# Two blocks of a retention layer loaded as 32x32 blocks and transposed on VectorE instead of TensorE

## The chip, the cores and the metric

The kernel runs on one core of a Trainium2 chip. A core has a matrix engine (TensorE, PE in the profile, with PEld for its weight loads), a vector engine (VectorE, DVE), a scalar engine (ScalarE, ACT), GpSimd (POOL) and a queue engine (SyncE, SP) that issues the transfers between HBM and the on-chip memory. Each engine runs its own instructions in the order of the program, and they wait for each other through semaphores. The metric is the device time of the launch in microseconds.

## The reference

q, k and v are float32 arrays of 8 batches x 8 heads x 576 positions x 64. For every batch and head

    ret = (q @ k.T / sqrt(64)) * D        D[i, j] = gamma_h ** (i - j) where i >= j, else 0
    attn = ret @ v

The heads are then laid side by side, which gives x with 4608 tokens of 512 numbers, and a feed-forward block follows:

    h = max(x @ w1, x @ w2, x @ w3)       512 -> 768
    out = h @ w_out                       768 -> 512

The four weights come as float64; they are made float32 on the chip.

## The kernel before

The 4608 tokens are cut into 36 blocks of 128 tokens (g = 0 to 35, C = 128) and 9 tiles of four blocks. The loop at the end of the kernel calls ffn(t), the feed-forward of tile t, and between its parts it puts the steps that steps(t + 1) lists for the blocks of the next tile. So while tile 0 goes through its feed-forward, blocks 4 to 7 go through the retention; the code calls these four a, b, c, d. That stretch is the one that the change touches. No scheduler moves anything: the order of the calls is the order on each engine.

**Tile 0's feed-forward.** The weights are loaded in 256 KB transfers as 64-bit words (`load_weights`, L610, tile name bits; the output weights L605 in transfers of 512 KB), two row groups to a buffer, with four buffers. `convert_all` turns each into float32: four ScalarE operations (L778, L779, L785, L788) and four VectorE operations (L786 frac, L791 mant, L795 expo, L803 w). The products come in nine units of two row groups (fp, i), called unit 0 to 8 here: each is 2 x 4 matmuls of 128x512 (`up_plain`, L934), followed by a maximum on VectorE (L939) or a copy on ScalarE (L941). Then come the products with w_out (L921). A float32 matmul shows as two instructions in the trace. When a buffer of words has been converted, it can be loaded again: the words of unit n + 4 wait for the conversion of unit n. Units 9 to 11 of this order are the output weights, called out0 to out2 here.

**Blocks 4 and 5 (a and b).** Their q, k and v are each loaded in 256 KB, or in two halves where a block lies across two batches, as block 4 does (L259). q and k are transposed on TensorE, 4 + 4 instructions a block (L295), and copied from PSUM by ScalarE (L296). `parity_scores` makes the scores of each half of 64 tokens on its own (L322) and the products of keys and values that carry the state from one half to the next (L327); VectorE masks the scores (L338) and sums the states (L346 to L350). `parity_values` takes the outputs from them (L506, L497); in the middle of it, two one-column copies on ScalarE (L510) stand between its first and its second group of products with the old states.

**Blocks 6 and later (c, d and on).** k is loaded twice: plainly (kraw), and with q in blocks of 32x32 (`load_blocks`, L241, tiles kxraw and qraw; 16 transfers of 32 KB a block, with runs of 128 bytes). VectorE transposes the 32x32 blocks, one instruction for k and one for q (L221, STREAM_TRANSPOSE). `chunk_scores` (L377, L380), a mask (L384), state sums on VectorE (L392) and GpSimd (L394) and `chunk_values` (L528, L535) do what the parity functions do for a and b, on other layouts of the same sizes. `carry` (L408) puts the state that the earlier form left into the layout of the later one.

**The queue.** Every load is issued by SP, in the order of the calls. The transfers of SP use eight semaphores in turn. The next transfer on a semaphore waits until the last one on it has landed, so a transfer cannot be issued before the one eight places ahead of it in the order has landed. An instruction that reads a tile waits for the semaphores of all the transfers that fill it; the transposes of a block's k and q wait for all 16.

Of the kernel before, what the change touches and what calls it, by code (L numbers as in the profile page):

```python
# [40 lines left out]
FP32 = mybir.dt.float32  # L41
# [10 lines left out]
NH = NT // 2  # L52
BY_PE = 6
BY_CHUNKS = 6
AHEAD = 3
# [44 lines left out]
def kernel(  # L100
# [23 lines left out]
    CPT = NT // C  # L124
    assert B * S % C == 0 and S % D == 0 and BY_CHUNKS % 2 == 0 and S >= C and N % NT == 0 and NT % P == 0 and 2 * D == P and NP == NDC

# [56 lines left out]
    assert all(start_of(g) in (0, None) for g in range(CPT))  # L183
    low = raw0.tile([P, D], FP32, name="low")
    for c in range(2):
        nc.gpsimd.tensor_copy(low[half(c)], causal[half(c), half(c)])


    raws, vds, qks, sts, states, mids, kvs, stacks = {}, {}, {}, {}, {}, {}, {}, {}

# [32 lines left out]
    def load_blocks(g, *blocks):  # L223
        for n, src in (("q", q), ("kx", k)):

            if 0 in blocks:
                shape = [P, NP, C // 32, 32] if g < BY_CHUNKS else [P, H, D // 32, 32]
                raws[n, g] = raw.tile(shape, FP32, tag=n, name=n + "raw", bufs=2)
            t = raws[n, g]
            for blk in blocks:  # L230
                b, pos = divmod(g * C + 32 * blk, S)
                if g < BY_CHUNKS:
                    for a in range(4):
                        nc.sync.dma_start(
                            t[32 * a:32 * a + 32, :, blk, :],
                            src[b, a // 2::2, pos:pos + 32, 32 * (a % 2):32 * (a % 2) + 32].rearrange("p j i -> j p i"))
                    continue
                c, e = divmod(blk, 2)
                for a in range(2):
                    r = D * c + 32 * a  # L240
                    nc.sync.dma_start(  # L241
                        t[r:r + 32, :, e, :],
                        src[b, :, pos:pos + 32, 32 * a:32 * a + 32].rearrange("h p i -> p h i"))
# [17 lines left out]
    def decay(g):  # L261
        factor = gk[:].unsqueeze(2).to_broadcast([C, H, D])
        t = raws.pop(("v", g))
        if spread or g >= CPT + 2:
            vds[g] = t
            scaling.extend(partial(nc.scalar.mul, t[:, h, :], t[:, h, :], gk[:, h:h + 1]) for h in range(H))
            return
        vds[g] = vpool.tile([C, H, D], FP32, tag="s", name="vd")
        engine = nc.gpsimd if g < CPT - 1 else nc.vector
        engine.tensor_tensor(vds[g][:], t[:], factor, op=ALU.mult)  # L270
# [4 lines left out]
    def transposes(g, names="kq"):  # L275
        both = qks.setdefault(g, {})
        if both:
            pass
        elif g >= BY_CHUNKS:
            for n, tag in (("k", "kT"), ("q", "m1")):  # L280
# [9 lines left out]
        for n in names:  # L290
            src = raws["k", g] if n == "k" else raws.pop(("q", g))
            pool, tag = (ps_r, "r") if g >= CPT else (ps_x, "x")
            pt = pool.tile([P, NP, C], FP32, tag=tag, name=n + "t")
            for p in range(NP):
                nc.tensor.transpose(pt[:, p, :], pair(src, p), ident[:C, :C])  # L295
            nc.scalar.copy(both[n][:], pt[:])  # L296

    def scores(g):
        chore(len(urgent))
        scale(len(scaling))  # L300
        if g >= CPT:
            (chunk_scores if g >= BY_CHUNKS else parity_scores)(g)
            return
# [6 lines left out]
        for j in range(2):  # L310
            st = sts[g, j] = att.tile([C, NP, C], FP32, tag=f"m{j}", name="st", bufs=2 + j)
            soon(partial(nc.vector.tensor_tensor, st[:], s[j][:],
                         causal[:].unsqueeze(1).to_broadcast([C, NP, C]), op=ALU.mult))

    def parity_scores(g):

        qT, kT, kr, vd = qks[g]["q"], qks[g]["k"], raws.pop(("k", g)), vds[g]
        rows = [ps_r.tile([P, 2, NP, D], FP32, tag="r", name=f"s{j}") for j in range(2)]
        kept = [c for c in range(2) if place(g, c) < S // D - 1]

        def score(p, j, c):
            nc.tensor.matmul(rows[j][half(c), 0, p, :], lhsT=kT[half(j), p, half(c)], rhs=qT[half(j), p, half(c)],  # L322
                             start=True, stop=True)

        def key_value(p, j, c):
            if c in kept:
                nc.tensor.matmul(rows[c][half(j), 1, p, :], lhsT=kr[half(c), 2 * p + j, :],  # L327
                                 rhs=vd[half(c), 2 * p + j, :], start=True, stop=True)

        for p in range(NP):  # L330
            for n in range(2):
                score(p, 0, n)
                score(p, 1, 1 - n)
                key_value(p, 1 - n, 0)
                key_value(p, n, 1)

        def mask(j):
            nc.vector.tensor_tensor(st[:, j::2, :], rows[j][:, 0], low[:].unsqueeze(1).to_broadcast([P, NP, D]),  # L338
                                    op=ALU.mult)

        def keep_parity(c):

            kv, factor = rows[c][:, 1], gs[:].unsqueeze(2).to_broadcast([P, NP, D])
            new = mids[g] if c == 0 else states[g + 1]
            if place(g, c) > 0:
                nc.vector.tensor_tensor(new[:], kv, (mids if c else states)[g][:], op=ALU.add)  # L346
                if c:
                    nc.vector.tensor_tensor(new[:], new[:], factor, op=ALU.mult)
            elif c:
                nc.vector.tensor_tensor(new[:], kv, factor, op=ALU.mult)  # L350
            else:
                nc.vector.tensor_copy(new[:], kv)

        st = sts[g] = att.tile([P, H, D], FP32, tag="m0", name="m", bufs=2)
        for j in range(2):
            soon(partial(mask, j))
        for c in kept:
            (states if c else mids)[g + c] = ppool.tile([P, NP, D], FP32, tag="part", name="state")
            soon(partial(keep_parity, c))

# [85 lines left out]
    def values(chunks, new_states=(), later=False, middle=()):  # L446
# [8 lines left out]
        if chunks[0] >= CPT:  # L455
            (chunk_values if chunks[0] >= BY_CHUNKS else parity_values)(chunks, t, i)
            return
# [27 lines left out]
        finish()  # L485

    def parity_values(chunks, t, i):
        o = [ps_r.tile([P, len(chunks), NP, D], FP32, tag="r", name="o") for _ in range(2)]
        cross = ((0, 0), (1, 1), (0, 1), (1, 0))

        def old(n):
            for b, g in enumerate(chunks):
                for u in range(0, NP, 2):
                    for j, c in cross:
                        m = j ^ n
                        if place(g, m) > 0:
                            nc.tensor.matmul(o[m][half(c), b, u + j, :],  # L497
                                             lhsT=(mids if m else states)[g][half(j), head(c, u) // 2, :],
                                             rhs=qks[g]["q"][half(j), head(c, u) // 2, half(m)],
                                             start=False, stop=True, skip_group_check=True)  # L500

        for b, g in enumerate(chunks):
            for u in range(NP):
                for m, c in cross:
                    h = head(c, u)
                    nc.tensor.matmul(o[m][half(c), b, u, :], lhsT=vds[g][half(m), h, :], rhs=sts[g][half(m), h, :],  # L506
                                     start=b == 0 and u == 0, stop=place(g, m) == 0, skip_group_check=True)
        old(0)
        for m in range(2):
            nc.scalar.copy(first[:], o[m][:, 0, 0, 0:1])  # L510

        def rest():
            old(1)
            between.append(partial(chunk_output, o, chunks, t, i))

        between.append(rest)

    def finish_values(_):
        between.pop()()

# [443 lines left out]
    def ffn(t):  # L964

        h = hpool.tile([P, NF, NT], FP32, tag="h", name="h")
        if t == 0:
            a, b, c, d = range(CPT, 2 * CPT)
            middles = {units[2]: [(transposes, a)], units[3]: [(scores, a)], units[5]: [(scores, b), (chunk_constants,)],
                       units[8]: [(transposes, d)]}  # L970
# [138 lines left out]
    def steps(t):  # L1109
# [12 lines left out]
        if t == 1:  # L1122
            a, b, c, d = range(CPT, 2 * CPT)
            at(0, (load, a, "kq"))
            at(1, (load, a, "v"))
            at(2, (load_weights, 2), (load, b, "kq"))
            at(3, (decay, a), (load, b, "v"), (load, c, "k"))
            at(4, (transposes, b), (load, c, "v"))
            at(5, (decay, b), (load, d, "kv"))
            at(6, (decay, c), (load_blocks, c, 0, 1, 2, 3))  # L1130
            at(7, (values, [a, b]), (finish_values, b), (decay, d), (convert, 2), (load_blocks, d, 0, 1, 2, 3))
            at(8, (transposes, c), (carry, c))
            at(9, (load, d + 1))
# [73 lines left out]
```

## Time and profile before

| | |
|---|---|
| median of 3 runs | 739.23 us (738.79 to 740.75) |
| the profiled execution | 738.46 us, with a span of 736.7 us |
| TensorE busy | 731.4 us, 99% of the span |
| VectorE busy | 572.3 us, 78% |
| ScalarE busy | 354.6 us, 48% |
| bytes moved | 59.38 MB, mean 81 GB/s |
| granted TensorE clock | 1.00 |

The page divides the span into 40 slices of 18.4 us and gives for each the busy share of each engine in tenths. The chain that ended last is followed back from the last instruction. A timeline lists instructions in the order of time: the start in us from the start of the span, how long they took, the engine, the line, what is written and read, and how many were merged into the row; in brackets stands the idle time of the engine before the row and what ended it. A row of SP tells how long the issue took, not the transfer. A table of windows gives for each stretch the busy time of each engine with the instructions begun in it, the granted clock, the busy share of the 16 DMA engines (over 1 where packets of one engine overlap) and the bytes per second.

### The profile page before, as it was taken

The numbers are of one execution on the slowest core, as the hardware profiler recorded it, in microseconds if no ns is written. First come the engines' busy times: TensorE is split into PE (matmuls) and PEld (weight loads), VectorE is DVE, ScalarE is ACT, GpSimd is POOL, SyncE is SP. The second block draws the span as 40 slices with busy tenths as digits, with TensorE's granted clock in tenths as the row PEclk, the third lists the DMA queues.
The fourth block names the chain that finished last, engine by engine and source line by source line (L and its number), as shares of the span: only waits on it lengthen the run. The fifth ranks groups of instructions, "written<-read, shape, count | busy, mean of one in ns | idle before, by whom it ended". The sixth has DMA issues, their size and how long they took to land.

```text
span 736.7 us, 17316 instructions
## 1 busy us (share of the span) xinstructions
PE 731.4 (99%) x6932; PEld 604.1 (82%) x6932; DVE 572.3 (78%) x1051; ACT 354.6 (48%) x740; POOL 39.1 (5%) x44
## 2 busy tenths in 40 slices
PE   9999999999999999999999999999999999999998
PEld 7654457888888888888888888888888888888887
DVE  5998799999886995689668866887768866893676
ACT  4886915444345525543364425543555245424441
POOL 2000010132000100010000000000100010000000
PEclk9999999999999999999999999999999999999999
DMA  9999554314251415151424243322514150000001
GB/s 222 264 233 247 107 98 115 67 27 91 73 100 27 91 42 105 37 97 32 103 52 79 45 109 60 64 53 64 109 29 88 46 125 6 1 31 28 1 1 57
DMA packets 233264, 59.38 MB, mean 81 GB/s; under 512 B 214496, under 2 KB 231904, under 8 KB 233184
## 3 DMA queue, kind: packets, MB, share of 16 engines
q1 hardware_dynamic: 232208, 58.24, 36.5%
q8 instruction: 54, 0.88, 0.5%
q14 instruction: 26, 0.21, 0.1%
q10 hardware_dynamic: 976, 0.04, 0.1%
HBM read 48.80 MB, written 9.44 MB: 79 GB/s over the span
## 4 chain that ended last, share of the span: by engine, by line
PE 97%; SPq 1%; DMA 1%; issue 0%; ACT 0%; DVE 0%
PE a L909 20%; PE b L909 17%; PE c L909 9%; PE up L934 9%; PE di L755 7%; PE d L909 6%; PE e L909 6%; PE dhc L755 5%; PE deg L755 3%; PE sk L377 3%; PE down L921 3%; PE o L528 2%; PE o L535 2%; PE dfd L755 2%; PE dx L662 1%; SPq L259 1%
## 5 line engine op out<-in xcount | busy, mean ns | idle before, releaser
L897 DVE TENSOR_TENSOR part<-part 128x512 f32<-128x512 f32 x168 | 117.9, 702 | 86.5 <-ACT part L894 83.9
L894 ACT COPY part<-b 128x512 f32<-128x512 f32 x120 | 70.3, 586 | 163.3 <-PE b L909 161.6
L897 DVE TENSOR_TENSOR h<-h,part 128x512 f32<-128x512 f32 x120 | 83.3, 694 | 24.0 <-ACT h L894 20.0
L894 ACT COPY part<-a 128x512 f32<-128x512 f32 x96 | 56.3, 586 | 51.6 <-PE a L909 51.1
L209 ACT ACTIVATE vraw<-vraw,gk 128x64 f32<-128x64 f32 x240 | 76.9, 347 | 6.6 <-DMA vraw<-in_v_dram 6.6
L909 PE MATMUL b<-s,n 128*128 128x256 f32 x288 | 73.9, 379 | 0.0
L934 PE MATMUL up<-xT,w 128*128 128x512 f32 (+2 forms) x160 | 63.5, 553 | 0.0
L909 PEld LDWEIGHTS b<-s,n 128*128 128x128 f32 x288 | 54.7, 190 | 7.4
L394 POOL TENSOR_TENSOR s<-s,gs_of 64x512 f32<-64x512 f32 x23 | 25.0, 1089 | 553.6 <-DVE s L392 476.5
L934 PEld LDWEIGHTS up<-xT,w 128*128 128x128 f32 x160 | 28.6, 190 | 30.1 <-issue 27.0
L909 PE MATMUL c<-xT,w 128*128 128x256 f32 x192 | 51.3, 389 | 0.0
L744 ACT COPY k<-di 128x256 f32<-128x256 f32 x49 | 18.3, 373 | 68.5 <-PE di L755 43.4
L909 PE MATMUL d<-s,w 128*128 128x256 f32 x192 | 49.8, 380 | 0.0
L909 PE MATMUL b<-xT,n 128*128 128x256 f32 x192 | 49.3, 379 | 0.0
L909 PE MATMUL a<-s,w 128*128 128x256 f32 x192 | 49.3, 379 | 0.0
L909 PE MATMUL a<-xT,w 128*128 128x256 f32 x192 | 49.3, 379 | 0.0
L909 PE MATMUL e<-xT,w 128*128 128x256 f32 x192 | 45.4, 379 | 0.0
L909 PE MATMUL a<-xT,n 128*128 128x256 f32 x192 | 45.4, 379 | 0.0
L909 PEld LDWEIGHTS e<-xT,w 128*128 128x128 f32 x192 | 36.5, 190 | 5.4 <-issue 0.5
L909 PEld LDWEIGHTS b<-xT,n 128*128 128x128 f32 x192 | 36.5, 190 | 5.0
L909 PEld LDWEIGHTS a<-s,w 128*128 128x128 f32 x192 | 36.5, 190 | 5.0
L909 PEld LDWEIGHTS a<-xT,w 128*128 128x128 f32 x192 | 36.5, 190 | 5.0
(196 smaller groups left out, 1382.1 us busy)
## 6 DMA issues: line engine op xcount, KB each, us to landing
bits<-in_moe_w_dram SPq DMA_DIRECT2D x36, 256.0 KB, 6.2
kraw<-in_k_dram SPq DMA_DIRECT2D x32, 256.0 KB, 3.1
vraw<-in_v_dram SPq DMA_DIRECT2D x32, 256.0 KB, 3.6
qraw<-in_q_dram SPq DMA_DIRECT2D x240, 32.0 KB, 2.1
kxraw<-in_k_dram SPq DMA_DIRECT2D x240, 32.0 KB, 2.1
out_dram<-osb SPq DMA_DIRECT2D x56, 128.0 KB, 1.7
bits<-in_moe_w_out_dram SPq DMA_DIRECT2D x6, 512.0 KB, 5.7
out_dram<-osb SPq DMA_DIRECT2D x7, 256.0 KB, 2.0
```

What stands on the lines that cost most here:

```text
L209: scaling.popleft()()
L377: nc.tensor.matmul(s[half(c), h, :], lhsT=kT[half(c), h, :], rhs=qT[half(c), h, :], start=True, stop=True)
L394: nc.gpsimd.tensor_tensor(new, new, factor, op=ALU.mult)
L528: nc.tensor.matmul(o[m][half(c), n, u, :], lhsT=vds[g][half(m), h, :], rhs=sts[g][half(m), h, :], start=n == 0 and u == 0, stop=place(g, m ...
L535: nc.tensor.matmul(o[m][half(c), n, u, :], lhsT=stacks[g][half(m), h, :], rhs=qks[g]["q"][half(m), h, :], start=False, stop=True, skip_gro ...
L744: nc.scalar.copy(place, a)
L755: nc.tensor.matmul(banks[chain], lhsT=hidden(h, order, b, late_ones)[:, e], rhs=late["V"][v][:, e], start=begins and e == 0, stop=chain no ...
L894: nc.scalar.copy(of[step], ps[step[0]][:])
L897: nc.vector.tensor_tensor(of[dst], a, b, op=op)
L909: nc.tensor.matmul(ps[chain][:, e, :], lhsT=factor(w, 2 * fp + e), rhs=xS[t][x], start=n == 1 and e == 0, stop=ends, skip_group_check=True)
L921: nc.tensor.matmul(b[:], lhsT=h[:, fb, m * P:(m + 1) * P], rhs=w_sb["out", fb], start=fb == blocks[0], stop=fb == blocks[-1])
L934: nc.tensor.matmul(ps[:, a:b], lhsT=w_sb[i, fb][:, dc * P:(dc + 1) * P], rhs=xT[t][:, dc, a:b], start=dc == 0 and a == 0, stop=dc == NDC - ...
```

## The change

Blocks 4 and 5 take the form of the later blocks. BY_PE goes from 6 to 4 and BY_CHUNKS goes away, and with it `parity_scores`, `parity_values` and what served them alone (the mask low, the dictionary mids, finish_values, one of the two load shapes). No new function is written: `load_blocks`, the VectorE transposes, `chunk_scores` and `chunk_values` now serve blocks 4 to 7 too. `carry`, from the state that block 3 leaves, is called for block 4 in place of block 6. The keys' decay of a and b is multiplied into the loaded tile itself; it stays one VectorE operation. In tile 0's feed-forward the scores of a move from unit 3 to unit 5, where those of b already stood, and now both stand between the two row groups of that unit; the small constants move from unit 5 to unit 2.

On the queue the order of the weights' loads among themselves is the same. What stands between them is moved: before, q, k and v of a and b were spread over four places; after, all of a's loads that are not k and v stand in one place, 16 transfers between the words of unit 4 and those of unit 5, and all of b's loads, k, v and 16 transfers, stand between the words of unit 7 and those of unit 8. The queue has 702 transfers in place of 673.

```diff
-BY_PE = 6
-BY_CHUNKS = 6
+BY_PE = 4
...
     def decay(g):
...
-        if spread or g >= CPT + 2:
+        if CPT <= g < CPT + 2:
+            vds[g] = t
+            nc.vector.tensor_tensor(t[:], t[:], factor, op=ALU.mult)
+            return
+        if g >= CPT:
...
     def scores(g):
...
-            (chunk_scores if g >= BY_CHUNKS else parity_scores)(g)
+            chunk_scores(g)
...
-            (chunk_values if chunks[0] >= BY_CHUNKS else parity_values)(chunks, t, i)
+            chunk_values(chunks, t, i)
...
-            middles = {units[2]: [(transposes, a)], units[3]: [(scores, a)], units[5]: [(scores, b), (chunk_constants,)],
+            middles = {units[2]: [(chunk_constants,)], units[3]: [(carry, a)], units[5]: [(scores, a, b)],
                        units[8]: [(transposes, d)]}
...
-            at(0, (load, a, "kq"))
-            at(1, (load, a, "v"))
-            at(2, (load_weights, 2), (load, b, "kq"))
-            at(3, (decay, a), (load, b, "v"), (load, c, "k"))
-            at(4, (transposes, b), (load, c, "v"))
-            at(5, (decay, b), (load, d, "kv"))
-            at(6, (decay, c), (load_blocks, c, 0, 1, 2, 3))
-            at(7, (values, [a, b]), (finish_values, b), (decay, d), (convert, 2), (load_blocks, d, 0, 1, 2, 3))
-            at(8, (transposes, c), (carry, c))
+            at(0, (load, a, "kv"))
+            at(1, (load_blocks, a, 0, 1, 2, 3))
+            at(2, (load_weights, 2))
+            at(3, (load, b, "kv"), (load_blocks, b, 0, 1, 2, 3), (decay, a))
+            at(4, (transposes, a))
+            at(5, (load, c, "kv"), (decay, b), (transposes, b))
+            at(6, (load, d, "kv"), (decay, c), (load_blocks, c, 0, 1, 2, 3))
+            at(7, (values, [a, b]), (decay, d), (convert, 2), (load_blocks, d, 0, 1, 2, 3))
+            at(8, (transposes, c))
```

More of the change, by code (lines that the diff above doesn't have):

```diff
@@ L124 @@
     CPT = NT // C
-    assert B * S % C == 0 and S % D == 0 and BY_CHUNKS % 2 == 0 and S >= C and N % NT == 0 and NT % P == 0 and 2 * D == P and NP == NDC
+    assert B * S % C == 0 and S % D == 0 and BY_PE == NT // C and S >= C and N % NT == 0 and NT % P == 0 and 2 * D == P and NP == NDC
     const = ctx.enter_context(tc.tile_pool(name="const", bufs=1))
@@ L183 @@
     assert all(start_of(g) in (0, None) for g in range(CPT))
[L184 to L189, printed above, removed]
+    raws, vds, qks, sts, states, kvs, stacks = {}, {}, {}, {}, {}, {}, {}
     def spans(g):
@@ L226, in load_blocks @@
             if 0 in blocks:
-                shape = [P, NP, C // 32, 32] if g < BY_CHUNKS else [P, H, D // 32, 32]
-                raws[n, g] = raw.tile(shape, FP32, tag=n, name=n + "raw", bufs=2)
+                raws[n, g] = raw.tile([P, H, D // 32, 32], FP32, tag=n, name=n + "raw", bufs=2)
             t = raws[n, g]
@@ L231, in load_blocks @@
                 b, pos = divmod(g * C + 32 * blk, S)
[L232 to L237, printed above, removed]
                 c, e = divmod(blk, 2)
@@ L278, in transposes @@
             pass
-        elif g >= BY_CHUNKS:
+        elif g >= BY_PE:
             for n, tag in (("k", "kT"), ("q", "m1")):
@@ L291, in transposes @@
             src = raws["k", g] if n == "k" else raws.pop(("q", g))
-            pool, tag = (ps_r, "r") if g >= CPT else (ps_x, "x")
-            pt = pool.tile([P, NP, C], FP32, tag=tag, name=n + "t")
+            pt = ps_x.tile([P, NP, C], FP32, tag="x", name=n + "t")
             for p in range(NP):
@@ L313, in scores @@
                          causal[:].unsqueeze(1).to_broadcast([C, NP, C]), op=ALU.mult))
[L315 to L359, printed above, removed]
     def begins(g):
@@ L485, in values @@
         finish()
[L487 to L519, printed above, removed]
     def chunk_values(chunks, t, i):
```

## The prediction

> **What bounds the kernel now.** First the page's chain that ended last: it is TensorE almost throughout.
>
> ```profile
> PE 97%; SPq 1%; DMA 1%; issue 0%; ACT 0%; DVE 0%
> ```
>
> Second the page's slices: TensorE is full from the second slice on, and the DMA engines are full through the first four (to 74 us), which is where blocks 4 and 5 are loaded.
>
> ```profile
> PE   9999999999999999999999999999999999999998
> DMA  9999554314251415151424243322514150000001
> ```
>
> Third TensorE's timeline of that stretch. Rows follow each other without idle time, so an instruction less is time won, and a wait is time lost.
>
> ```profile
> 40.32 0.60 PE L295 MATMUL kt<-ident,kraw 128*128 128x128 f32 x4
> 40.76 0.60 PE L295 MATMUL qt<-ident,qraw 128*128 128x128 f32 x4
> 41.20 7.03 PE L934 MATMUL up<-xT,w 128*128 128x512 f32 x16
> ...
> 64.05 0.27 PE L322 MATMUL s<-qT,kT 64*64 64x64 f32 x2
> ...
> 76.62 0.64 PE L497 MATMUL o<-qT,state 64*64 64x64 f32 x24
> 77.53 0.68 PE L497 MATMUL o<-qT,state 64*64 64x64 f32 x24 [0.27 <-ACT first L510]
> ```
>
> The 0.27 is the only wait there. Fourth the queue and its transfers. Eight loads of q blocks take 5.58 us to issue when they stand behind large loads, because each waits for the transfer eight places ahead; the eight of kx behind them take 3.90, 0.49 each, and land 2.1 us after their issue (second fence, asked for 71 to 75 us). A 256 KB load on an emptied queue takes about 3 us (third, 96.5 to 97.9 us). The last line is the windows' row for 36 to 48 us: a full DMA moves 252 GB/s.
>
> ```profile
> 35.93 6.81 SPq L610 DMA_DIRECT2D bits<-in_moe_w_dram  x8
> ...
> 65.47 5.58 SPq L241 DMA_DIRECT2D qraw<-in_q_dram  x8
> 71.09 3.90 SPq L241 DMA_DIRECT2D kxraw<-in_k_dram  x8
> ```
>
> ```profile
> kxraw<-in_k_dram SPq DMA_DIRECT2D x8, 32.0 KB, 2.1
> ```
>
> ```profile
> kraw<-in_k_dram SPq DMA_DIRECT2D x1, 256.0 KB, 2.9
> ```
>
> ```profile
> 36.00:48.00 12.00, 12.00 (x35) 5.58 (x33) 11.19 (x15) 11.94 (x13) 0.00 (x0) 1.00 1.14 252
> ```
>
> Last VectorE: two idle times where it waits for TensorE, and what a transpose pair costs (0.63 + 0.67, from start to start).
>
> ```profile
> 57.29 0.69 DVE L939 TENSOR_TENSOR h<-h,up 128x512 f32<-128x512 f32 x1 [2.62 <-PE up L934]
> ...
> 60.72 0.69 DVE L939 TENSOR_TENSOR h<-h,up 128x512 f32<-128x512 f32 x1 [0.81 <-PE up L934]
> ...
> 86.67 0.70 DVE L221 STREAM_TRANSPOSE kT<-kxraw 128x512 f32<-128x512 f32 x1
> 87.30 0.67 DVE L221 STREAM_TRANSPOSE qT<-qraw 128x512 f32<-128x512 f32 x1
> ```
>
> **The change part by part.** *TensorE, won.* The transposes of a and b go: 40.32 to 41.20 and 52.78 to 53.65, 1.76 us. Scores: parity took 48.16 to 49.24 and 64.05 to 65.14, 2.17; two chunk scores, c and d, took 92.07 to 94.11, 2.04; 0.13 won. Outputs: parity_values took 75.64 to 78.14, 2.50 with its wait; chunk_values took 101.18 to 103.20, 2.02; 0.48 won. Together 2.37 us.
>
> *ScalarE* loses four copies of 0.59 and the two of 0.16; carry (0.80) moves. *VectorE* gains two pairs of transposes, 2.6 us; masks and states of a and b cost 3.23 before (0.76 + 0.41 + 0.76 + 0.88 + 0.42) and about 3.48 after (0.69 + 0.69, 0.69 + 1.41). These 2.9 us fit into the 3.4 us of idle time above; without that cover they would cost at most as much. *GpSimd* gains one product of about 1 us (L394), with 75 us idle before its first. The decay is the same 0.68 us. All these I take as nothing.
>
> *The queue: when do b's blocks land?* A 256 KB load takes 262,144 B / 252 GB/s = 1.04 us. The weight load issued at 23.18 landed 7.1 later, at 30.3. After the change: k and v of a, 512 KB, to 32.4; six weight loads to 38.6; now a's eighth q block waits for the last of these, and eight kx at 0.49 follow it, to 42.5. In that time the queue of bytes runs empty. The next weight load is issued at 43.0 and lands 3.0 later, 46.0; eleven more to 57.4; k and v of b to 59.5; its eighth q block waits for that, eight kx to 63.4, landing at 65.5. The same reckoning of the order before gives 60.5 for the last weight load of units 0 to 8; issued at 56.48, it landed 5.3 later, at 61.8. So I add the 1.3 that it falls short: 66.8. VectorE's transposes of b: 68.1.
>
> *The first wait.* TensorE comes to the scores of b at 64.05 - 1.76 - 1.08 (a's scores, no longer at unit 3) + 1.02 (now just ahead) = 62.2. It waits 68.1 - 62.2 = 5.9 us. Behind the waiting transpose on VectorE stand the last steps of unit 6's weights (1.22 + 1.23, ready at 70.6); TensorE wants them after b's scores and half a unit (1.0 + 3.5), at 72.6: covered. Before this, unit 5's weights land at about 50.4 and are ready about when TensorE comes for them (60.52 - 2.84 = 57.7); a wait there would come off the 5.9, not on top.
>
> *The second wait.* Behind b's blocks stand unit 8's weights, out0, k and v of c, out1, k and v of d, c's blocks, out2, d's blocks. With kx of b issued at 64.7: a weight load at 65.2 lands at 68.2, three more at 71.3. Then 3.15 MB at 315 GB/s (the windows' 60 to 70 us, with such loads): 81.3. c's eight kx: 85.2. out2's second load, issued at 86.1, lands 4.9 later as before (75.53 to 80.46): 91.0. d's eight kx 94.9, landed 97.0, transposed 98.3. TensorE comes to the scores of d at 92.07 - 2.37 + 5.9 + 1.0 = 96.6, and waits 1.7. Before, d was transposed at 91.7 for 93.05.
>
> Later, VectorE is full from 95 to 134 us. The product at 117.90 reads a sum that ended at 115.69, 2.2 us of room; VectorE comes out of d's transposes 6.6 late and TensorE 5.2, so 0.8 is left. Nothing is added.
>
> Sum: -2.37 + 5.9 + 1.7 = +5.2. The profiled execution took 738.46 (736.7 and 1.8 around it): 743.7. It stands 0.8 below the median, against which I predict 744.4.
>
> *Ends.* First wait: at 276 GB/s (20 to 30 us), 0.09 less for each of 22 loads, and without the 1.3: 2.6; at 234 (30 to 35 us): 7.7. I take 252, the stretch of the same loads. Second: zero, if out2 and d come in time; at 252 GB/s for the 3.15 MB, 4.2. Sum from +0.2 to +9.5.
>
> *A rule against it.* The granted clock is 1.00 in every slice, and after 16 us no wait of TensorE is over 0.3 us; so no row shows what a long one does. The Trainium skill, TensorE: Matmul & The Clock Gate, section "What's actually happening", says that an idle window of about 3.4 us halves the clock until a busy window of that length. By that, an estimate from this page, the first wait could cost up to 1.7 us more; no run here shows it yet, and the sum leaves it out.
>
> **Rivals.** *Hidden: faster.* If b's last block landed by 60.9 (62.2 less 1.3) and d's in time, only the 2.37 would show: 736.1 against the profile, 736.9 against the median. The price turns at that landing, 5.9 us sooner. For it: small loads could overtake large ones. Against it: c's first seven q blocks, issued behind out1, took 3.7 us to land at the median in place of 2.1; and the twelve weight loads would have to come at 0.6 us each, 430 GB/s, where the best five microseconds of the trace (60 to 65) show 335.
>
> *One wait alone: about even.* With the low end of the first wait and none at d: 739.4. For it: 276 GB/s was seen with weights alone. Against it: at 36 to 48, weights nearly alone, it was 252.
>
> *More waits: over +8.* A DMA at 234 GB/s lengthens both waits: about 748.7. For it: a gap like that at 30 to 35 us may come again; the 128-byte runs may slow the weights. Against it: the queue holds only eight transfers, so the small ones pass between.
>
> **How the numbers follow.** Both waits 0.60; one wait or small ones 0.18; more 0.13; hidden 0.09. A measurement tells 0.3%, 2.2 us, from no change. Hidden is faster: 0.09. Of "one wait", 0.10 lies within 0.3%, and 0.01 of the likeliest: same 0.11. Slower 0.80. The likeliest's own range is 741.5 to 747. The range takes the ends, +0.2 to +9.5: 739.4 to 748.7; it leaves out the hidden case and what is beyond, under 2 in 10.
>
> **What would show it.** Right: L295 gone after 20 us; SP's timeline with 16 block loads between the weights and a DMA share well under 1 in their second half, at about 40 to 45 and 60 to 64 us; VectorE idle some 5 us before a transpose of kx, released by a DMA; TensorE idle 3 to 7 us before L322 of the new file at 62 us, and up to 4 at about 96. Wrong: TensorE without a gap there, or the DMA full through 40 to 65 us, which would put b's blocks earlier; a granted clock under 1 would add what the sum leaves out.

## The result and the profile after

The changed kernel takes 750.98 us at the median of six runs (750.34 to 754.35) against 739.24 us for the kernel before (738.71 to 740.75): a ratio of 1.0171, with a 95% interval from 1.0157 to 1.0186. It is 11.7 us slower; the prediction was +5.2, and its range ended at 748.7.

The profiled execution took 754.35 us with a span of 752.3 us, 15.6 more than the span before. It is one of the two longest of the six; the other four spans lie between 748.3 and 749.2 us. First the page's slices and its chain that ended last.

```profile
PE   8996979999999999999999999999999999999998
...
PEclk9998989999999999999999999999999999999999
DMA  9987753513242424332342325141515151001001
...
PE 91%; SPq 3%; DVE 3%; DMA 2%; issue 1%; ACT 0%; DVEq 0%
```

A slice is 18.8 us. TensorE is no longer full in the fourth and the sixth (56 to 75 and 94 to 113 us), the granted clock falls in the same two, and the chain now passes through SP's queue and VectorE. From the first product of tile 1 to the last matmul both kernels take 616.5 us. Of the 15.6 us, 15.0 lie in tile 0: from its first product of the feed-forward to the first of tile 1 it is 96.35 us before and 111.36 after. Most of the rest is that the stretch begins 0.3 us later (21.02 in place of 20.68).

Next TensorE's waits (us in total, times, longest) and, from its timeline, the three rows that waited over 0.5 us in that stretch.

```profile
PE sk L322 <- DVE qT L216: 8.1, 2, 5.3
PE up L845 <- ACT mant L690: 2.9, 1, 2.9
```

```profile
60.86 6.73 PE L845 MATMUL up<-xT,w 128*128 128x512 f32 x8 [2.86 <-ACT mant L690]
...
71.48 0.27 PE L322 MATMUL sk<-qT,kT 64*64 64x64 f32 x2 [2.81 <-DVE qT L216]
...
105.46 0.48 PE L322 MATMUL sk<-qT,kT 64*64 64x64 f32 x4 [5.29 <-DVE qT L216]
```

It waits for the weights of unit 5, for b and for d. VectorE's timeline tells what these were waiting for: the words of unit 5, which it could begin at 52.38 and had made into weights at 60.7, and the block loads of b and of d.

```profile
52.38 0.69 DVE L697 TENSOR_SCALAR frac<-bits 128x1024 int32<-128x1024 int32 x1 [2.91 <-DMA bits<-in_moe_w_dram]
...
59.48 1.23 DVE L714 TENSOR_TENSOR w<-mant,expo 128x1024 f32<-128x1024 f32 x1
...
70.12 0.71 DVE L216 STREAM_TRANSPOSE kT<-kxraw 128x512 f32<-128x512 f32 x1 [5.68 <-DMA kxraw<-in_k_dram]
...
104.01 0.71 DVE L216 STREAM_TRANSPOSE kT<-kxraw 128x512 f32<-128x512 f32 x1 [5.93 <-DMA qraw<-in_q_dram]
```

So all three are late loads. SP's timeline shows the queue, and the windows what the DMA engines did meanwhile (the last two numbers of a row are their busy share and GB/s, the one before is the granted clock). In both fences the first row is of the kernel before, the others are of the changed one.

```profile
81.89 3.77 SPq L241 DMA_DIRECT2D kxraw<-in_k_dram  x8
...
35.30 5.33 SPq L229 DMA_DIRECT2D qraw<-in_q_dram  x8
40.68 4.41 SPq L229 DMA_DIRECT2D kxraw<-in_k_dram  x8
45.20 7.92 SPq L521 DMA_DIRECT2D bits<-in_moe_w_dram  x12
...
57.57 6.48 SPq L229 DMA_DIRECT2D qraw<-in_q_dram  x8
64.09 3.90 SPq L229 DMA_DIRECT2D kxraw<-in_k_dram  x8
68.09 2.59 SPq L521 DMA_DIRECT2D bits<-in_moe_w_dram  x4
...
80.16 7.11 SPq L229 DMA_DIRECT2D qraw<-in_q_dram  x8
87.32 3.90 SPq L229 DMA_DIRECT2D kxraw<-in_k_dram  x8
...
97.25 4.98 SPq L229 DMA_DIRECT2D kxraw<-in_k_dram  x8
```

```profile
40.00:45.00 5.00, 5.00 (x19) 2.62 (x18) 4.46 (x6) 4.97 (x7) 0.00 (x0) 1.00 1.09 248
...
35.00:40.00 5.00, 5.00 (x13) 2.28 (x12) 4.79 (x8) 4.93 (x7) 0.00 (x0) 1.00 1.16 239
40.00:45.00 5.00, 5.00 (x13) 2.13 (x12) 4.47 (x6) 4.93 (x7) 0.00 (x0) 1.00 0.37 57
45.00:50.00 5.00, 5.00 (x13) 2.23 (x12) 4.44 (x5) 0.61 (x1) 0.00 (x0) 1.00 0.79 179
```

While SP issues a's block loads, the engines fall from 239 to 57 GB/s, where they moved 248 before, and they need until 50 us to fill again. The queue's last row is d's kx: SP had issued d's kx by 85.7 us before (81.89 + 3.77) and does so by 102.2 now (97.25 + 4.98), 16.6 us later.

Last the clock, in windows of 1 us around its changes.

```profile
60.00:61.00 1.00, 0.14 (x1) 0.17 (x2) 1.00 (x2) 1.00 (x2) 0.00 (x0) 0.59 1.28 283
61.00:62.00 1.00, 1.00 (x2) 0.48 (x3) 0.91 (x2) 0.97 (x2) 0.00 (x0) 0.50 1.04 212
66.00:67.00 1.00, 1.00 (x3) 0.34 (x1) 0.00 (x0) 0.97 (x2) 0.00 (x0) 0.50 0.44 68
67.00:68.00 1.00, 1.00 (x26) 0.49 (x27) 0.00 (x0) 0.39 (x1) 0.00 (x0) 1.00 0.44 68
104.00:105.00 1.00, 0.00 (x0) 0.00 (x0) 0.99 (x2) 0.00 (x0) 0.00 (x0) 0.78 0.48 73
...
111.00:112.00 1.00, 1.00 (x3) 0.48 (x2) 0.51 (x2) 0.00 (x0) 0.50 (x1) 0.81 0.48 105
```

TensorE ran at half clock twice, for 6.8 us each (60.2 to 67.0 and 104.6 to 111.4). The ledger of the stretch is then: waits 10.96 in place of 0.27, +10.7; work at full clock about 94.5 in place of 96.1, -1.6 (the 94.5 is that of the last experiment, 95.42 less 0.91 of waits); the rest, 111.36 - 10.96 - 94.5 = 5.9, is what the two halvings cost in busy time. Sum +15.0. The 94.5 is borrowed from another kernel with the same products, so the split between the last two terms is an estimate.

### The profile page after: what moved, and what is told of

It reads as the page before. It is cut to its first block, busy times and chain, and to the rows that moved or that the text cites. A ratio compares the mean times of both kernels' runs of the same rounds, so it can differ in the third digit from the quotient of the medians.

```text
span 752.3 us, 17312 instructions
## 1 busy us (share of the span) xinstructions
PE 735.9 (98%) x6916; PEld 605.6 (81%) x6916; DVE 575.8 (77%) x1052; ACT 351.8 (47%) x734; POOL 38.3 (5%) x43
## 4 chain that ended last, share of the span: by engine, by line
PE 91%; SPq 3%; DVE 3%; DMA 2%; issue 1%; ACT 0%; DVEq 0%
PE a L820 19%; PE b L820 17%; PE c L820 9%; PE di L666 6%; PE d L820 6%; PE e L820 6%; PE dhc L666 5%; PE up L845 5%; PE deg L666 3%; PE down L832 3%; PE sk L322 3%; PE o L439 2%; PE o L446 2%; SPq L229 2%; PE dfd L666 2%; PE dx L573 1%
## 5 line engine op out<-in xcount | busy, mean ns | idle before, releaser
L845 PE MATMUL up<-xT,w 128*128 128x512 f32 (+2 forms) x160 | 66.2, 574 | 2.9 <-ACT mant L690 2.9
L845 PEld LDWEIGHTS up<-xT,w 128*128 128x128 f32 x160 | 29.8, 197 | 36.3 <-issue 29.6
L322 PEld LDWEIGHTS sk<-qT,kT 64*64 64x64 f32 x1024 | 32.1, 137 | 14.8 <-issue 11.5
L322 PE MATMUL sk<-qT,kT 64*64 64x64 f32 x1024 | 34.6, 223 | 8.1 <-DVE qT L216 8.1
L820 PEld LDWEIGHTS a<-xT,n 128*128 128x128 f32 x192 | 36.5, 190 | 5.0
```

What stands on the lines that cost most here:

```text
L322: nc.tensor.matmul(s[half(c), h, :], lhsT=kT[half(c), h, :], rhs=qT[half(c), h, :], start=True, stop=True)
L820: nc.tensor.matmul(ps[chain][:, e, :], lhsT=factor(w, 2 * fp + e), rhs=xS[t][x], start=n == 1 and e == 0, stop=ends, skip_group_check=True)
L845: nc.tensor.matmul(ps[:, a:b], lhsT=w_sb[i, fb][:, dc * P:(dc + 1) * P], rhs=xT[t][:, dc, a:b], start=dc == 0 and a == 0, stop=dc == NDC - ...
```

## The experiments

The theory that the result suggests: each block load holds SP's queue about half a microsecond, all that stands behind is later by the sum, and TensorE waits and is slowed where the lateness comes out. Each run is compared with runs of the kernel before on the same chip (738.98 to 739.51 us).

**The half clock: e1_fill.** Products of three row groups are made twice, as filling for the waits.

```diff
-            for dc in range(NDC):
+            for dc in list(range(NDC)) * (2 if (t, fb, i) in TWICE else 1):
...
+TWICE = ((0, 3, 1), (0, 2, 2), (0, 5, 2))
```

> The changed kernel with the products of three row groups made twice, the same result written again: the second row group of unit 4 (ahead of the wait for the words of unit 5), the first of unit 5 (ahead of the scores of b) and the last of unit 8 (ahead of the scores of c and d). That is 3 x 3.5 us of work more on TensorE, put where it waited 2.9, 2.8 and 5.3 us. Theory: what ends the waits (b's blocks, d's blocks) is set by the loads, so the work fits in; the half clock at 60 us costs nothing by itself, since TensorE waits for b after it anyway; the half clock at 105 us costs up to 3.4 us and goes, because its idle window is filled. 747 to 749 in every run, clock 1.00. Rival, each halving of the clock costs its 3.4 us: about 745. Rival, the clock is not what costs: 751 to 754, or more by what does not fit.

Measured 751.81 us, 1.0174 (1.0149 to 1.0198): not the 747 to 749 that the theory gave, but what the rival gave by which the clock is not what costs. Its profiled execution has a span of 749.5 us and a clock of 1.00 throughout, and can be laid beside that of the changed kernel, because its loads came at the same time.

```profile
71.41 0.27 PE L323 MATMUL sk<-qT,kT 64*64 64x64 f32 x2 [1.73 <-DVE qT L217]
...
105.47 0.33 PE L323 MATMUL sk<-qT,kT 64*64 64x64 f32 x4 [1.92 <-DVE qT L217]
```

With 7.0 us more of work ahead of them b's scores begin at 71.41 (71.48 without), and with 10.5 us more d's begin at 105.47 (105.46). In the profiled execution of the changed kernel the first halving thus cost nothing: TensorE would have waited for b that much longer. The second cost the difference of the spans, 2.8 us, since it went on behind the start of d's scores. In the medians this does not show. Four of the changed kernel's runs had a mean clock of 0.993 to 0.995, where the profiled one had 0.991, so they hold less half clock than it; and where loads land earlier, the filling no longer fits into the waits. The latter is argued, not shown.

**The place or the form: e2_place.** The kernel before, its loads of a and b put where the changed kernel has them, in the old form. Its TensorE transposes and its scores of a move to units 4 and 5 as well.

```diff
-            at(0, (load, a, "kq"))
-            at(1, (load, a, "v"))
-            at(2, (load_weights, 2), (load, b, "kq"))
...
+            at(0, (load, a, "kv"))
+            at(1, (load, a, "q"))
+            at(2, (load_weights, 2))
+            at(3, (load, b, "kvq"), (decay, a))
```

> The kernel before, with its old form of blocks 4 and 5 (256 KB loads, TensorE transposes, parity functions), but with their loads where the changed kernel has them: k and v of a first, q of a between the words of units 4 and 5, k, v and q of b between the words of units 7 and 8; both scores in unit 5, a's transposes in unit 4, b's in unit 5. Theory (the 16 small loads in one place let the queue of bytes run empty, the place alone does not): the words of unit 5 land some 6.6 us sooner than in the changed kernel and d's blocks some 13 sooner, no wait of TensorE over 1 us, 738 to 741. Rival (the place decides: what is behind the weights comes too late in any form): waits at b's transposes and at d as in the changed kernel, 745 or more.

Measured 740.28 us, 1.0012 (1.0002 to 1.0021). This is TensorE's longest wait after 20 us:

```profile
PE s L322 <- ACT qT L296: 0.7, 1, 0.7
```

The place is not the cause.

**The loads by themselves: e8_idle and e11_few.** The kernel before, with 29 block loads that nobody reads, as many as the changed kernel has more; in the second, of 4 KB each (`0:1` in place of the full range of heads).

```diff
+            nc.sync.dma_start(unused[r:r + 32, :, m // 2 % 2, :],
+                              src[b, :, pos:pos + 32, 32 * a:32 * a + 32].rearrange("h p i -> p h i"))
...
+            at(1, (load, a, "v"), (idle_loads, a, 16))
...
+            at(3, (decay, a), (load, b, "v"), (load, c, "k"), (idle_loads, b, 13))
```

> The kernel before with 29 block loads of 32 KB into a tile that nobody reads, 16 behind a's v (between the words of units 4 and 5) and 13 behind c's k: as many as the changed kernel has more. Theory (the loads by their number on SP's queue make the loss): all behind comes 13 to 15 us later, d's transposes at 104 to 106 in place of 91.7, a wait of TensorE at c and d of 9 to 13 us in all, 748 to 753. Rival (the loss comes from what the loads are wanted for, b's transposes holding up VectorE): 739 to 742.

> The kernel before with 29 idle loads as in the run with 29 idle block loads, but of 4 KB in place of 32 KB (one head in place of eight, 32 runs of 128 bytes): the same number, an eighth of the runs and bytes. Theory (a load costs SP's queue its issue whatever it moves): still about half a us each, TensorE late by 9 us or more, 747 to 756. Rival (runs and bytes cost the DMA engines their time): an eighth of the loss, 739 to 742.

With 32 KB: 755.88 us, 1.0219 (1.0203 to 1.0234), 16.4 us more, above the 748 to 753 of the theory. With 4 KB: 751.97 us, 1.0185 (1.0169 to 1.0200), 13.0 more. Idle loads alone thus make a loss as large as the change's, and an eighth of the bytes still makes four fifths of it. TensorE waits for b and for d, first with 32 KB, then with 4 KB:

```profile
60.27 1.09 PE L304 MATMUL kt<-ident,kraw 128*128 128x128 f32 x4 [6.44 <-DMA kraw<-in_k_dram]
107.66 0.37 PE L386 MATMUL sk<-qT,kT 64*64 64x64 f32 x2 [4.87 <-DVE qT L221]
...
57.30 0.63 PE L304 MATMUL kt<-ident,kraw 128*128 128x128 f32 x4 [3.79 <-DMA kraw<-in_k_dram]
102.60 0.34 PE L386 MATMUL sk<-qT,kT 64*64 64x64 f32 x4 [2.40 <-DVE qT L221]
```

SP's timeline and the window of the 4 KB run show why:

```profile
36.15 5.36 SPq L251 DMA_DIRECT2D unused<-in_q_dram  x8
41.55 3.67 SPq L251 DMA_DIRECT2D unused<-in_k_dram  x8
```

```profile
40.00:45.00 5.00, 5.00 (x19) 2.73 (x18) 4.46 (x7) 5.00 (x6) 0.00 (x0) 1.00 0.06 9
```

Eight loads of 4 KB hold the queue 3.67 us, 0.46 each; eight of 32 KB held it 3.90. The DMA engines are 6% busy meanwhile. It is mainly the number of loads on the queue; what they move makes the other 3.4 us.

**Spread between the weights: e4_spread.** Two block loads behind each of 16 transfers of weights.

```diff
+                    if g in SPREAD:
+                        little.append((g, step))
...
                     nc.sync.dma_start(blocks[half(c)], heads[:, head(c, 0):head(c, NP)])
+                    some(PER)
```

> The changed kernel with the 32 block loads of a and b issued two behind each of the next 16 transfers of weights, from the words of unit 4 on, in place of 16 and 16 in one place. Theory (the DMA runs empty while 16 small loads are issued 0.49 us apart and refills in 3.8 us): the DMA stays near 250 GB/s from 30 to 60 us, the words of unit 5 come 3 us sooner, b's last block lands at 61 to 65 in place of 69.9, waits of TensorE under 3 us together; 737 to 742. Rival (small runs cost the DMA as much wherever they stand): b's last block at 68 to 70, 748 to 751.

Measured 748.85 us (746.70 to 754.86), 1.0139 (1.0092 to 1.0185). The theory's number is missed; the median lies in the rival's 748 to 751, but not for the rival's reason. In the profiled execution, the slowest of the four, b's last block landed at 64.7, as the theory had it. What came late was b's v, issued behind all the blocks; its decay on VectorE stands ahead of b's transposes:

```profile
68.64 0.69 DVE L265 TENSOR_TENSOR vraw<-vraw,gk 128x512 f32<-128x512 f32 x1 [4.06 <-DMA vraw<-in_v_dram]
```

The theory had left out that the queue itself is then the bound:

```profile
33.65 0.60 SPq L534 DMA_DIRECT2D bits<-in_moe_w_dram  x1
34.30 1.09 SPq L205 DMA_DIRECT2D qraw<-in_q_dram  x2
35.49 0.60 SPq L534 DMA_DIRECT2D bits<-in_moe_w_dram  x1
```

A group of one transfer of weights and two block loads takes 1.8 us to issue, where the weights alone landed 1.085 us apart in the changed kernel. The engines stay at 146 to 195 GB/s from 40 to 65 us; nothing is gained by the spreading but the emptiest moments.

**Later readers: e3_later.** b's transposes one step and b's scores one unit later.

```diff
-units[5]: [(scores, a, b)],
+units[5]: [(scores, a)], units[6]: [(scores, b)],
...
-            at(5, (load, c, "kv"), (decay, b), (transposes, b))
-            at(6, (load, d, "kv"), (decay, c), (load_blocks, c, 0, 1, 2, 3))
+            at(5, (load, c, "kv"), (decay, b))
+            at(6, (transposes, b), (load, d, "kv"), (decay, c), (load_blocks, c, 0, 1, 2, 3))
```

> The changed kernel with b's VectorE transposes one step later and b's scores in unit 6 in place of unit 5; the loads stand where they did. Theory (b's transposes, waiting for their blocks, hold up VectorE's conversion of unit 6, and through the buffer of words out1's load and d's blocks behind it): no wait at b, 3 us won there, d's blocks some 3 to 5 us sooner and d's wait down from 5.3 to 1 to 3.5; 743 to 747. Rival (DMA alone sets d's blocks): only b's wait goes, d's grows by as much: 750 to 751. Rival (the wait moves to unit 6's weights): 751.

Measured 754.44 us, 1.0194 (1.0172 to 1.0217), above every range given. The theory fell, and the waits are those of the first rival: b's is gone, and d's has taken most of it over. In the profiled execution, the fastest of the four at 752.10 us, the waits are 10.2 us in all in place of 10.96; what the other three lost is not shown.

```profile
61.36 6.63 PE L845 MATMUL up<-xT,w 128*128 128x512 f32 x8 [3.42 <-ACT mant L690]
...
104.69 0.48 PE L322 MATMUL sk<-qT,kT 64*64 64x64 f32 x4 [6.78 <-DVE qT L216]
```

d's blocks came 0.8 us sooner (transposes at 103.2 in place of 104.0), not 3 to 5: VectorE's wait at b is not what makes them late. I had thought that VectorE, waiting for b, keeps a buffer of words and through it out1's load. In the changed kernel that load was issued from 74.66 for 3.87 us, and the profile names VectorE as what released it; here VectorE came to unit 6's words 6.5 us earlier (64.87 in place of 71.35), and the load went out at nearly the same time (74.17, 3.36 long). What holds it is open.

**Another queue: e5_pool, e6_pool4, e7_act.** GpSimd issues the block loads of a and b, then those of a to d; or ScalarE those of a and b.

```diff
-                    nc.sync.dma_start(
+                    (nc.gpsimd if g in (4, 5) else nc.sync).dma_start(
```

> The changed kernel with the 32 block loads of a and b issued by GpSimd in place of SP; nothing else. Theory (each block load holds SP's queue some 0.5 us whatever its size, and all that stands behind is later by the sum): SP's queue is 16 us of issues shorter, so unit 5's words land by about 46, d's blocks are transposed near 92, and b's by the time GpSimd has issued them (a's from 25 us on, if about 1 us each, b's to about 57, landed by 60); waits of TensorE under 1.5 us together, 736.5 to 738.5, faster than before. Rival (the small runs cost the DMA engines their time, whichever queue issues them): the same waits at b and d as in the changed kernel, 748 to 751. Rival (GpSimd issues too slowly): only b late, 740 to 745.

> As the run with GpSimd issuing for a and b, and c's and d's 32 block loads too. Theory: SP's queue is shorter by another 16 us before d; nothing of d can be late; 736 to 738. If a and b alone already take the waits away, no difference between the two beyond 0.5 us. Rival (GpSimd's sums of states, L339, which stand behind its loads, come late): waits at the outputs of a and b or of c and d, 739 to 743.

> The changed kernel with the 32 block loads of a and b issued by ScalarE. Theory: SP is relieved as with GpSimd, but each issue takes ScalarE some 0.5 us, 8 us for a and 8 for b, in the stretch where it converts words and was 95% busy; the conversions of units 3 to 6 come late by some of that: 738 to 746. Rival (cost lies in the DMA engines): 748 to 751.

By GpSimd 744.01 us, 1.0054 (1.0042 to 1.0066), and 743.95 us, 1.0055 (1.0038 to 1.0072), not the 736 to 738.5 expected. Some 7 of the 11.7 us come back, and nothing more with c and d. What is left are mostly waits for words, since GpSimd issued from 16.9 us on and its loads took DMA time from the words of early units: the load of words that lands at 32.1 us in the changed kernel (issued at 23.89) lands at 35.8 here. The rows are of the run with a and b alone:

```profile
31.53 14.00 PE L845 MATMUL up<-xT,w 128*128 128x512 f32 x32 [1.29 <-DVE w L714]
48.03 17.43 PE L845 MATMUL up<-xT,w 128*128 128x512 f32 x40 [2.51 <-DVE w L714]
95.66 0.33 PE L322 MATMUL sk<-qT,kT 64*64 64x64 f32 x4 [0.63 <-DVE qT L216]
```

By ScalarE 754.47 us, 1.0204 (1.0191 to 1.0217), outside what any theory gave. Its timeline shows the 16 issues of a in the midst of the conversions, and what they cost:

```profile
33.38 3.85 ACTq L229 DMA_DIRECT2D qraw<-in_q_dram  x8
37.27 5.94 ACTq L229 DMA_DIRECT2D kxraw<-in_k_dram  x8
43.60 0.66 ACT L689 ACTIVATE expo<-bits 128x512 f32<-128x512 bf16 x1 [9.51 <-DMA kxraw<-in_k_dram]
```

I had counted 8 us of issues; it is 9.8, and two of the second eight begin only as an earlier load lands (39.88 behind a landing at 39.85, 42.39 behind one at 42.37). ScalarE converts nothing meanwhile, the same comes again at b, and TensorE waits 6.7 and 5.9 us for weights.

**Towards a better version: e9_gate, e10_best, e12_a.** GpSimd's loads of a and b behind a one-column copy that reads unit 1's maximum; then with b's readers as in the run with later readers, c's loads by GpSimd and d's on SP ahead of out2's words; then with a's transposes one step later (the last three lines below, against the run before).

```diff
+    def after_unit_1():
+        nc.gpsimd.tensor_copy(first[:], late["h"][:, 0, 0:1])
...
-            at(1, (load_blocks, a, 0, 1, 2, 3))
-            at(2, (load_weights, 2))
+            at(2, (load_weights, 2), (load_blocks, a, 0, 1, 2, 3), (load_blocks, b, 0, 1, 2, 3))
...
-            at(4, (transposes, a))
-            at(5, (load, c, "kv"), (decay, b))
+            at(5, (transposes, a), (load, c, "kv"), (decay, b))
```

> The changed kernel with a's and b's 32 block loads issued by GpSimd, but only behind a one-column copy on GpSimd that reads the first maximum of unit 1 (at about 35 us), in place of 17 us. Theory (issued from 17 us on they took DMA time from the words of units 1 and 3, for which TensorE then waited 1.3 and 2.5 us; the words of later units have room): those two waits go, b's last block lands at 60 to 63, a wait of 0 to 3 us at b's scores, none over 1 at d: 737 to 741. Rival (the DMA engines have 4 to 5 us more to move before b's scores wherever the loads stand): the same 744 as without the copy.

> As the run with the copy ahead of GpSimd's loads, and: b's VectorE transposes one step and b's scores one unit later, c's block loads by GpSimd too, d's on SP one step earlier, ahead of out2's words. Theory: no block is late any more, TensorE waits for nothing over 1 us, and its 2.4 us of saved work show: 736 to 738.5, faster than both kernels. Rival (words of units 3 to 6 come late by the DMA's 4 to 5 us more): 739 to 743.

> As the run with GpSimd's loads, b later and d earlier, with one more step moved: a's VectorE transposes stand one step later, behind the last two operations on unit 5's words in place of ahead of them. Theory (VectorE waited 5.2 us for a's q blocks with unit 5's words behind it, and TensorE 2.4 us for these): the wait of 2.4 goes, a's scores come 0 to 1 us late at most, 736.5 to 738, faster than the kernel before. Rival (the wait moves to a's scores): 738.5 to 740, as without the step moved.

With the copy alone 748.39 us, 1.0124 (1.0110 to 1.0138), slower than without it, and above what either theory gave. Both early waits went, but unit 5's words then stood on VectorE behind a's transposes (2.6 us for TensorE), and GpSimd took from 36.3 to 64.4 us for the 32 loads. That is 0.88 each, in place of the 0.58 of a load that nothing holds, because each waits for the one eight places ahead and these now land after 6.6 to 7.0 us. TensorE waited 5.9 us for b. With the readers moved 739.60 us, 1.0010 (0.9999 to 1.0022), in its rival's range, and one wait of 2.4 us was left: VectorE waited for a's blocks with unit 5's words behind. With that order turned round:

```profile
PE sk L327 <- DVE qT L216: 0.7, 1, 0.7
PE o L451 <- issue: 0.2, 1, 0.2
```

These are all waits that remain in the stretch, which takes 95.42 us in place of 96.35. The time is 738.73 us, 0.9995 (0.9986 to 1.0004): not to be told from the kernel before, and 0.7 us above the 736.5 to 738 expected. The profiled spans are equal (736.7 us): the stretch begins 0.5 us later than before (21.18 in place of 20.68), and what follows it takes 0.4 more; no run explains either.

## Why the prediction was right or wrong

- **Sign and mechanism: right.** The loads came late, behind a queue that small loads held, and the DMA engines ran empty where the prediction put it (40 to 45 us, share 0.37) and again behind b's (62 to 70 us, 0.37 to 0.45). The idle loads show that such loads are enough for it.
- **The first wait: right in sum by luck, late in time.** Predicted 5.9 us at b; it came as 2.86 at unit 5's weights and 2.81 at b, 5.67 together. But half clock lay between the two, and TensorE began b's scores at 71.48, not at 68.1. The term that was too small is when b's last block lands: 66.8 reckoned, 69.9 measured. SP came to unit 5's words at 45.20 in place of 43.0, and 1.7 us of this were there before any block load: the last weights ahead of the blocks landed at 40.3 in place of 38.6. The reckoning had started from a load that landed at 30.3 in the one profiled execution before; the same load landed at 32.1 in the changed kernel and at 31.4 to 33.0 in the ten other runs that have the same loads ahead of it. Unit 5's first load then took 3.75 us to land in place of 3.0, and the twelve landed 1.085 us apart in place of 1.04. And the issue of b's q blocks was not hidden: the eighth was out at 64.05, 1.7 us after b's v had landed.
- **The second wait: wrong, and the step that failed.** Predicted 1.7 us, measured 5.29. d's blocks were transposed at 105.3 in place of 98.3, while TensorE was only 3.6 us later than reckoned. Of the 7 us, 4.2 were there when unit 8's words had landed (75.5 in place of 71.3: b's 3.1 and a slower filling), the large loads behind won 0.7 back, and c's blocks lost 2.5. I took the issue of c's q blocks as hidden behind the large loads, as it was at a. It ran from 80.16 to 87.28, 2.5 us past the landing of the last large load (84.81): SP reached them at 80.16 and needed 2.73 us for the first, and the profile does not show what held it. out2's words and d's own blocks took 0.6, and the transposes began 0.4 after d's last landing.
- **The sum of the miss.** In the profiled execution d's scores began at 105.46 in place of 98.3, 7.2 us late, and the clock behind them cost 2.8: 10.0 of the 10.2 us by which tile 1 began later than predicted (132.4 in place of 117.0 + 5.2). The median is 6.6 us above the prediction; the executions near it were not profiled.
- **The half clock: left out of the sum, and it cost 5.9 us of busy time in the profiled execution, of which 2.8 reached the end.** The prediction's estimate from the Trainium skill, TensorE: Matmul & The Clock Gate, section "What's actually happening", was 1.7 us for one wait, half clock for one window of about 3.4 us; the trace has 6.8 us at half clock at each of two. The section's idle window of about 3.4 us is also longer than the idle time ahead of the first fall, 2.2 us (58.0 to 60.2). That section also says that the window is free-running; the two falls lie 44.4 us apart, 13 windows of its 3.413 us, which fits.
- **The gain: about right.** Predicted 2.4 with a wait of 0.27 in it, so 2.1 of work; by the last experiment's trace the work of the stretch fell by 1.6 us.
- **Work taken as nothing.** GpSimd and VectorE had room: in the last experiment, with the same work, TensorE waits 0.9 us in all. `carry` did not quite: its 0.84 us on ScalarE stood at 55.0 us among the conversions of unit 5 for which TensorE then waited. That it lengthened that wait is read from the order alone.
- **The rivals.** "More waits" was nearest, with 748.7 and a chance of 0.13; its slower DMA was there (1.085 us for 256 KB is 242 GB/s), but the larger part was the chain from b to d and the clock. "Hidden" was far off: it wanted b's last block at 60.9.

## What to carry to other kernels

Price a transfer on a full queue by its issue first: splitting a load into eight costs what the queue needs for seven more, here 0.46 to 0.49 us each whether they move 4 or 32 KB, and the transfers behind are later by about the sum (d's kx by 16.6 us behind 29 more loads). Follow that sum to the last consumer on the queue, not only to the first: making the first reader wait less moved most of its wait to the next one. A reckoning that starts from a landing in one execution carries that execution's luck with it, here 1.7 us. GpSimd's queue had room and brought the loss back, though no gain, when its loads were held until the earlier ones had had the DMA engines, and when the readers stood behind work that was ready.

## What the runs showed of the hardware that I had not expected

- A load of 4 KB and one of 32 KB hold SP's queue about the same time: 0.46 and 0.49 us.
- A wait of 2.86 us was enough to halve TensorE's clock, 2.2 us after TensorE fell idle at 58.0; a wait of 2.81 us ten microseconds later was not. With the idle loads of 4 KB the clock fell at 58.4 us, 1.1 us after a wait of 3.79 us had ended at 57.3 (the granted clock is 0.71 from 58 to 59 us). Each halving of the changed kernel lasted 6.8 us, each of that run 3.4.
- The same nine transfers of weights landed 0.95 us apart in the profiled execution before (22.7 to 30.3 us) and 1.03 apart after (23.9 to 32.1). The change does not touch what stands ahead of them, and no run explains it.
